# The MLP's second product, two token tiles at a time on the array's upper and lower 64 rows

## The chip, the cores and the metric

The kernel runs on one core of one Trainium2 chip. The metric is the device time of one execution, in microseconds. The kernel before takes 744.76 us, the median of three runs that lie between 744.68 and 744.93.

## The reference

Four layers act on `x` of 2048 tokens and 576 features, in bfloat16: linear attention (A), MLP (B), and both again with the same weights. Each adds to its input what it makes of the input's layer norm.

```python
def _B_ref(x, w1, b1, w2, b2):          # D = 576, F = 4608
    y = _layernorm(x, axis=-1)
    h = _gelu(jnp.einsum("bsd,df->bsf", y, w1) + b1)
    return jnp.einsum("bsf,fd->bsd", h, w2) + b2

x = x + _A_ref(_layernorm(x, axis=-1), A_wqkv, A_wo)
x = x + _B_ref(_layernorm(x, axis=-1), B_w1, B_b1, B_w2, B_b2)
x = x + _A_ref(_layernorm(x, axis=-1), A_wqkv, A_wo)
x = x + _B_ref(_layernorm(x, axis=-1), B_w1, B_b1, B_w2, B_b2)
```

The attention has 32 heads of 18 features. It takes keys, values and queries as products of `y` with `wqkv`, `phi(t) = where(t > 0, t + 1, exp(t)) + 1e-6` of keys and queries, sums keys times values over all tokens, and multiplies each query with that sum, over a denominator, and with `wo`.

## The kernel before

All weights stay in SBUF (`w1_sb`, `w2_sb` and so on; the profile calls both of the MLP's `w_sb`). Tokens stand in 16 tiles of 128; four tiles make a chunk of 512. The order on each engine is the order in which the program issues, kept by hand: `mm` (L228) chains TensorE's matmuls, and wrappers do the same for VectorE (`vec`), ScalarE (`act`), GpSimd (`pool`) and SyncE's DMA queue (`sp`). All TensorE work but the transposes is therefore under L229 in the profile, and all of the other engines' under L53; tiles tell the groups apart.

An MLP layer is `LayerB.run` (L1217). For each of four chunks it does:

- **The first product**, nine `m1_group`s (L1175) of four blocks of 128 hidden features. It works on half arrays: a matmul contracts over 64 partitions only, on the upper or the lower 64 rows of the array, and one of each half runs at the same time. 576 features are nine halves. `row_tiles` (L231) interleaves the two streams: the upper half takes the group's four sums in the order 0, 1, 2, 3, the lower half in the order 2, 3, 0, 1. The two halves must not write one PSUM bank at a time, so a bank passes from one to the other only after a *relay*, a tiny instruction on another engine (`relay_by_act`, a copy on ScalarE; or `relay_by_pool`, a memset on GpSimd) that waits for the last matmul of one half and is waited for by the first of the other. ScalarE's GELU writes a block into `units`, a buffer of 37 slots of 128 x 512; slot f is `hT[f]`. The sums 0 and 2 stand in a pair of banks (`hp_ps`, tags accA and accB in turn), the sums 1 and 3 in single banks (`h_ps`, tags one0 to one3 in turn).
- **The second product**, L1240 to L1277: tile by tile, 36 x 2 matmuls on the full array. The weights are a slot's 128 tokens (128 x 128), the moving operand is half a row of `w2_sb` (288 columns), and the result is `m_ps`, a pair of banks (two single banks, one2 and one3, for the last tile of a layer).

Between and beside these:

- `residual` (L546) adds the two halves to `xo`, the tile's `x` plus the bias, in one VectorE instruction. `bias_rows` (L537) makes `xo` on GpSimd; there is one buffer of it.
- `lnq` is a queue of layer norms for the next chunk's first product (kind B) and, where an attention follows, for the tiles just finished (kind A). `feed` puts a tile in, and each `tick` issues the next of four steps for every tile in it: statistics (VectorE), reciprocal root (GpSimd), the norm (VectorE, its padding on GpSimd), transposition through `shared` (VectorE, then after the fourth tile 16 DMAs into `yT`). Kind A also writes its rows to DRAM (`y_rows`).
- The second attention begins right after the first MLP layer with `lower_tails` (L652), which loads small tails into slots 17 and 18 of `units`; a GpSimd memset over slots 3 to 16; `placed_rows` (L496), DMAs of 12 tiles' rows into slots 3 to 16; `k_batch` (keys of two tiles) and `q_batch`, both with relays on GpSimd; and `key_rows` (L723), which needs a tile's rows as weights.
- `wo_pair` (L1025), an attention's last product, also works on half arrays, on two tiles at a time, with 288 columns.

In the second product, the full-array loop is:

```python
for f in range(NF):
    for half in range(2):
        mm(acc[half], hT[f][:, j * P:(j + 1) * P],
           w2_sb[:, f, half * HALF:(half + 1) * HALF], f == 0, f == NF - 1)
    if f % 12 == 6:
        while fed < {6: TPC - 1, 18: TPC}.get(f, 0):
            feed_next(c, fed)
            fed += 1
        lnq.tick()
```

The last tile of the last layer is computed as 384 and then 192 columns, so that the first part can be written out early.

Of the kernel before, what the change touches and what calls it, by code (L numbers as in the profile page):

```python
# [8 lines left out]
ALU = mybir.AluOpType  # L9
# [6 lines left out]
P = 128  # L16
NT = S // P
KD = 5
DPAD = KD * P
NF = F // P  # L20
# [6 lines left out]
NCB = S // CB  # L27
TPC = CB // P
CA = 512
NCA = S // CA  # L30
HALF = D // 2
# [4 lines left out]
def build(tc, A_x, A_wqkv, A_wo, B_w1, B_b1, B_w2, B_b2, out, n_layers=4):  # L36
    nc = tc.nc
    with ExitStack() as ctx:
# [23 lines left out]
        vec, act = InOrder(nc.vector, "VectorE"), InOrder(nc.scalar, "ScalarE")  # L62
        pool, sp = InOrder(nc.gpsimd, "GpSimd"), InOrder(nc.sync, "SyncE")

        x_in = A_x.flatten_outer_dims()
        out_f = out.flatten_outer_dims()
# [6 lines left out]
        def pair(name, tag=None):  # L73
            if tag is None:
                pair_turn["n"] += 1
                tag = ("accA", "accB")[pair_turn["n"] % 2]
            return ps_pair.tile([P, 2, 512], F32, name=name, tag=tag)
# [3 lines left out]
        def one_tag():  # L81
            one_turn["n"] += 1
            return f"one{one_turn['n'] % one_turn['banks']}"

        def one(name, tag=None):
            return ps_one.tile([P, 512], F32, name=name, tag=tag or one_tag())
# [106 lines left out]
        w2_sb = const.tile([P, NF, D], BF16, name="w2_sb")  # L193
        b1T = const.tile([P, NF], F32, name="b1T")
        b2_bc = const.tile([P, D], BF16, name="b2_bc")
        x_sb = const.tile([P, NT, D], BF16, name="x_sb")
# [25 lines left out]
        def pe(inst):  # L222
            if pe_last["last"] is not None:
                tc.add_manual_dep(inst.ins, pe_last["last"], NOSYNC, reason="TensorE order")
            pe_last["last"] = inst.ins.name
            return inst

        def mm(out_, lhsT, rhs, start, stop, **kw):  # L228
            return pe(nc.tensor.matmul(out_, lhsT=lhsT, rhs=rhs, start=start, stop=stop, **kw))  # L229

        def row_tiles(ops_of, dst, relay, after):  # L231


            order = [(hi, op) for step in zip([op for n in (0, 1, 2, 3) for op in ops_of(n, 0)],
                                              [op for n in (2, 3, 0, 1) for op in ops_of(n, 1)]) for hi, op in enumerate(step)]
            first, final, total = {}, {}, [0] * 4
            for i, (hi, (n, _, _)) in enumerate(order):
                first.setdefault((hi, n), i)
                final[(hi, n)] = i
                total[n] += 1  # L240
            relay_at = {max(final[(0, a)], final[(1, b)]): (a, b) for a, b in ((0, 2), (1, 3))}
            starts = {first[(1, 0)]: 0, first[(0, 2)]: 2, first[(1, 1)]: 1, first[(0, 3)]: 3}
            relay_of, seen = {}, [0] * 4
            for i, (hi, (n, wt, mv)) in enumerate(order):
                ins = mm(dst[n], wt, mv, seen[n] == 0, seen[n] == total[n] - 1)
                seen[n] += 1
                if i in starts:
                    tc.add_manual_dep(ins.ins, relay_of[starts[i]], SYNC, reason="row tiles take turns on a PSUM bank")
                if i in relay_at:
                    passed = relay()  # L250
                    tc.add_manual_dep(passed.ins, ins.ins.name, SYNC, reason="row tiles take turns on a PSUM bank")
                    for m in relay_at[i]:
                        relay_of[m] = passed.ins.name
                after(n, [a == b for a, b in zip(seen, total)], relay_at.get(i))
# [254 lines left out]
        class Queue:  # L509
# [3 lines left out]
            def feed(self, t, kind, eng="dve", transpose="dma"):  # L513
                n = Norm(t, kind, eng, transpose)
                self.items.append([n.stats, n.rstd, n.norm, n.transposed])
# [11 lines left out]
        lnq = Queue()  # L527

        def warm_table(func):
            act.activation(out=act_dummy[:, 0:1], in_=neg_half[:, 0:1], func=func)  # L530

        def two(ap):
            return ap.rearrange("p (h n) -> p h n", h=2)

        xo_of = {}

        def bias_rows(t):  # L537
            xo = work.tile([P, D], F32, name="xo", tag="xo", bufs=1)
            add = pool.tensor_tensor(out=xo[:], in0=x_sb[:, t, :], in1=b2_bc[:], op=ALU.add)
            if t == 0:  # L540
                tc.add_manual_dep(add.ins, gate["after"], SYNC, reason="not beside the attention's rows")
            xo_of[t] = xo
# [3 lines left out]
        def residual(li, t, halves):  # L546
            xo = xo_of.pop(t)[:] if t in xo_of else x_sb[:, t, :]
            vec.tensor_tensor(out=two(x_sb[:, t, :]), in0=halves, in1=two(xo), op=ALU.add)
            if li == n_layers - 1:
                sp.dma_start(out=out_f[t * P:(t + 1) * P, :], in_=x_sb[:, t, :])  # L550
# [619 lines left out]
        class LayerB:  # L1170
# [41 lines left out]
            def flush(self):  # L1212
                if self.held is not None:
                    self.held()
                    self.held = None

            def run(self):  # L1217
                li, next_kind = self.li, self.next_kind

                def feed_next(c, i):  # L1220
                    if c + 1 < NCB:
                        lnq.feed((c + 1) * TPC + i, "B")

                for c in range(NCB):

                    fed = 0
                    for g in range(self.done, NGRP):
                        self.m1_group(c, g)
                        if g in ((8,) if c == 0 else (5, 7)):
                            feed_next(c, fed)  # L1230
                            fed += 1
                        if g == (8 if c == 0 else 7):
                            bias_rows(c * TPC)
                        lnq.tick()
                    self.flush()
                    if c == NCB - 1 and next_kind == "A":
                        warm_table(ACT.Exp)
                    hT = self.hT.pop(c)
                    self.done = 0
                    for j in range(TPC):  # L1240
                        t = c * TPC + j
                        if t == NT - 1 and li == n_layers - 1:
                            for cols in (slice(0, 384), slice(384, D)):
                                width = cols.stop - cols.start
                                acc = one("m2_ps")
                                for f in range(NF):
                                    mm(acc[:, 0:width], hT[f][:, j * P:(j + 1) * P], w2_sb[:, f, cols],
                                       f == 0, f == NF - 1)
                                vec.tensor_tensor(out=x_sb[:, t, cols], in0=acc[:, 0:width],
                                                  in1=xo_of[t][:, cols], op=ALU.add)  # L1250
                                sp.dma_start(out=out_f[t * P:(t + 1) * P, cols], in_=x_sb[:, t, cols])
                            break
                        if t == NT - 1:

                            acc = [one("m2_ps", tag)[:, 0:HALF] for tag in ("one2", "one3")]
                        else:
                            both = pair("m2_ps")[:, :, 0:HALF]
                            acc = [both[:, half, :] for half in range(2)]
                        for f in range(NF):
                            for half in range(2):  # L1260
                                mm(acc[half], hT[f][:, j * P:(j + 1) * P],
                                   w2_sb[:, f, half * HALF:(half + 1) * HALF], f == 0, f == NF - 1)
                            if f % 12 == 6:
                                while fed < {6: TPC - 1, 18: TPC}.get(f, 0):
                                    feed_next(c, fed)
                                    fed += 1
                                lnq.tick()
                        if t == NT - 1:
                            for half in range(2):
                                cols = slice(half * HALF, (half + 1) * HALF)  # L1270
                                vec.tensor_tensor(out=x_sb[:, t, cols], in0=acc[half], in1=xo_of[t][:, cols], op=ALU.add)
                        else:
                            residual(li, t, both)
                        if j + 1 < TPC:
                            bias_rows(t + 1)
                        if next_kind == "A":
                            lnq.feed(t, "A")  # L1277

        kinds = ["A", "B", "A", "B"][:n_layers]

# [153 lines left out]
```

## Time and profile before

| | |
|---|---|
| median of three runs | 744.76 us (744.68 to 744.93) |
| the profiled execution | 745.07 us |
| its span, first to last instruction | 743.4 us |
| TensorE matmuls busy | 737.0 us, 6942 instructions |
| TensorE weight loads busy | 479.2 us, 6951 instructions |
| VectorE, ScalarE, GpSimd busy | 268.8, 297.3, 131.7 us |
| `m_ps` (second product): matmuls of 128 x 288 | 2216 of `units` and 16 of `pk`, mean 286 ns, and 72 of 384 and 192 columns |
| `h_ps` and `hp_ps` (first product) | 2592 of 64 x 512, mean 376 ns |
| `m_ps` in the chain that ended last | 38% of the span |

The profile gives a matmul's duration from its start to the modelled end of its results, so neighbours overlap: the mean of one is not the time between two. The time between two is had from starts, or from the length of a stretch over its count. The chain (section 4 of the page) follows the work that ended last back from the end; listed in order of time it shows stretches of the same work with start, length and count. Form `64*128` means a weight tile of 64 rows and 128 columns, half the array; `128*128` is the full array.

### The profile page before, as it was taken

The numbers are of one execution on the slowest core, as the hardware profiler recorded it, in microseconds if no ns is written. First come the engines' busy times: TensorE is split into PE (matmuls) and PEld (weight loads), VectorE is DVE, ScalarE is ACT, GpSimd is POOL, SyncE is SP. The second block draws the span as 40 slices with busy tenths as digits, with TensorE's granted clock in tenths as the row PEclk, the third lists the DMA queues.
The fourth block names the chain that finished last, engine by engine and source line by source line (L and its number), as shares of the span: only waits on it lengthen the run. The fifth ranks groups of instructions, "written<-read, shape, count | busy, mean of one in ns | idle before, by whom it ended". The sixth has DMA issues, their size and how long they took to land.

```text
span 743.4 us, 16663 instructions
## 1 busy us (share of the span) xinstructions
PE 737.0 (99%) x6942; PEld 479.2 (64%) x6951; DVE 268.8 (36%) x674; ACT 297.3 (40%) x642; POOL 131.7 (18%) x403
## 2 busy tenths in 40 slices
PE   8999999999999999999999999999999999999998
PEld 4666557774576457646777665777646754774476
DVE  7868735433025302400365685452401040100000
ACT  5666743007601740374035666320373047106700
POOL 4541000422022201200213120021300120010010
PEclk9999999999999999999999999999999999999999
DMA  7956220022011202110023001202000200020000
GB/s 197 240 161 210 66 86 17 16 46 44 2 27 42 38 1 45 36 26 1 17 85 85 28 1 38 67 1 53 18 1 9 52 10 1 18 44 9 1 10 24
DMA packets 61297, 34.74 MB, mean 47 GB/s; under 512 B 37126, under 2 KB 61222, under 8 KB 61222
## 3 DMA queue, kind: packets, MB, share of 16 engines
q1 hardware_dynamic: 60470, 33.45, 17.8%
q8 instruction: 54, 0.88, 0.5%
q10 hardware_dynamic: 752, 0.23, 0.2%
q14 instruction: 21, 0.17, 0.1%
HBM read 21.70 MB, written 4.93 MB: 36 GB/s over the span
## 4 chain that ended last, share of the span: by engine, by line
PE 98%; DVE 1%; DMA 1%; SPq 0%; issue 0%; DVEq 0%
PE m_ps L229 38%; PE hp_ps L229 20%; PE h_ps L229 17%; PE k_ps L229 5%; PE q_ps L229 5%; PE wo_ps L229 5%; PE rk_ps L229 4%; PE tp L468 1%; PE side_ps L229 1%; DMA x_sb<-in_A_x_dram 1%; SPq L53 0%; PE den_ps L229 0%; PE kvwo_ps L229 0%; PE kv_ps L229 0%; PE rden_ps L229 0%; DVE pk L53 0%
## 5 line engine op out<-in xcount | busy, mean ns | idle before, releaser
L229 PEld LDWEIGHTS <-units 128*128 128x128 bf16 (+1 forms) x2926 | 267.4, 97 | 66.4 <-issue 3.6
L229 PE MATMUL m_ps<-w_sb,units 128*128 128x288 bf16 (+2 forms) x2288 | 283.0, 286 | 0.0
L229 PEld LDWEIGHTS <-w_sb 64*128 64x128 bf16 x2304 | 129.2, 94 | 129.8 <-issue 2.1
L229 PE MATMUL h_ps<-yT,w_sb 64*128 64x512 bf16 x1152 | 173.7, 376 | 0.0
L229 PE MATMUL hp_ps<-yT,w_sb 64*128 64x512 bf16 x1152 | 151.5, 376 | 0.0
L53 DVE TENSOR_TENSOR x_sb<-m_ps,xo 128x576 bf16<-128x576 f32 (+3 forms) x34 | 24.4, 721 | 323.6 <-PE m_ps L229 323.6
L53 ACT ACTIVATE units<-hp_ps,b1T 128x512 bf16<-128x512 f32 x144 | 91.2, 684 | 86.4 <-PE hp_ps L229 86.4
L53 ACT COPY relay_sb<-relay_sb 128x1 f32<-128x1 f32 x112 | 21.4, 191 | 235.7 <-PE hp_ps L229 225.0
L53 ACT ACTIVATE units<-h_ps,b1T 128x512 bf16<-128x512 f32 x142 | 95.2, 687 | 0.0
L53 POOL TENSOR_TENSOR xo<-x_sb,b_bc 128x576 f32<-128x576 bf16 x32 | 40.8, 1274 | 302.9 <-DVE x_sb L53 291.5
L229 PE MATMUL k_ps<-wkv_sb,yT 64*128 64x288 bf16 (+3 forms) x432 | 61.0, 299 | 0.6 <-ACT yT L53 0.5
L229 PE MATMUL hp_ps<-yT,w_tail 64*128 64x512 bf16 x144 | 54.1, 376 | 0.0
L229 PE MATMUL h_ps<-yT,w_tail 64*128 64x512 bf16 x144 | 54.1, 376 | 0.0
L53 DVE BATCH_NORM_STATS2 ln_st<-x_sb 128x6 f32<-128x288 bf16 x128 | 51.3, 441 | 1.4 <-DMA x_sb<-in_A_x_dram 1.1
L53 DVE STREAM_TRANSPOSE shared<-y_ring 128x640 bf16<-128x640 bf16 x40 | 32.9, 826 | 41.4 <-DMA yT<-shared 39.3
L53 ACT ACTIVATE phi_e<-k_ps 128x288 bf16<-128x288 f32 x64 | 26.3, 413 | 53.7 <-PE k_ps L229 50.0
L229 PEld LDWEIGHTS <-yT 64*128 64x128 bf16 (+1 forms) x448 | 36.3, 95 | 9.2 <-ACT yT L53 0.8
L229 PE MATMUL q_ps<-yT,wq_sb 64*128 64x512 bf16 (+2 forms) x273 | 40.4, 347 | 0.4
L53 DVE TENSOR_SCALAR y_ring<-x_sb,ln_mv,ln_rstd 128x576 bf16<-128x576 bf16 (+2 forms) x60 | 30.3, 506 | 24.5 <-POOL ln_rstd L53 24.3
L53 POOL MEMSET pool_relay<- 128x1 f32 x152 | 16.7, 110 | 125.3 <-PE hp_ps L229 43.6
L229 PE MATMUL wo_ps<-shared,units 64*128 64x288 bf16 (+1 forms) x480 | 38.1, 283 | 0.1
L229 PEld LDWEIGHTS <-w_tail 64*128 64x128 bf16 x288 | 27.1, 94 | 16.7
(110 smaller groups left out, 500.4 us busy)
## 6 DMA issues: line engine op xcount, KB each, us to landing
yT<-shared SPq DMA_DIRECT2D x160, 40.0 KB
w_sb<-in_B_w_dram SPq DMA_DIRECT2D x12, 432.0 KB
w_sb<-in_B_w_dram SPq DMA_DIRECT2D x9, 512.0 KB
yT<-rden_rows SPq DMA_DIRECT2D x24, 126.0 KB
y_rows<-y_ring SPq DMA_DIRECT2D x16, 144.0 KB
units<-y_rows SPq DMA_DIRECT2D x16, 144.0 KB
x_sb<-in_A_x_dram SPq DMA_DIRECT2D x15, 144.0 KB
out_dram<-x_sb SPq DMA_DIRECT2D x15, 144.0 KB
```

Of the source, the lines that this page charges most:

```text
L53: inst = issue(*args, **kw)
L229: return pe(nc.tensor.matmul(out_, lhsT=lhsT, rhs=rhs, start=start, stop=stop, **kw))
L468: pe(nc.tensor.transpose(out=tp[:, k - a, :], in_=self.y[:, k * P:(k + 1) * P], identity=ident[:]))
```

## The change

The second product runs through `row_tiles` too: a new `two_tiles` takes tiles t and t + 1 together. Sum n is tile n % 2 and column half n // 2; each sum is made of 36 matmuls on the upper and 36 on the lower 64 rows, so that a call has 288 half-array matmuls in four quarters, with two relays on ScalarE. The even tile's two sums stand in a pair of banks and are complete after three quarters; its residual is issued there. The odd tile's stand in two single banks and are complete at the end; they are added in two VectorE instructions. The `lnq` feeds and ticks are counted in matmuls of a call. In the last call of a layer, slots 17, 18 and 3 to 16 are read first, and its ticks stand at other places. In the last chunk of the last layer only the first two tiles are paired; the other two stay as they were.

```diff
+            def two_tiles(self, c, j, hT, feed):
+                li, t = self.li, c * TPC + j
+                both = pair("m2_ps")
+                tags = ("one2", "one3") if t + 2 == NT else (None, None)
+                early = [one("m2_ps", tag) for tag in tags]
+                dst = [both[:, 0, 0:HALF], early[0][:, 0:HALF], both[:, 1, 0:HALF], early[1][:, 0:HALF]]
+                step = dict(n=0)
+                early_slots = [17, 18] + list(range(3, 17)) if t + 2 == NT else []
+                order = early_slots + [f for f in range(NF) if f not in early_slots]
+
+                def ops_of(n, hi):
+                    at, rows, cols = (j + n % 2) * P, slice(64 * hi, 64 * hi + 64), slice(n // 2 * HALF, (n // 2 + 1) * HALF)
+                    return [(n, hT[f][rows, at:at + P], w2_sb[rows, f, cols]) for f in order]
+
+                def after(n, done, turn):
+                    step["n"] += 1
+                    if step["n"] == 72:
+                        feed()
+                    if step["n"] % 48 == 24 and (step["n"] < 216 or t + 2 < NT):
+                        lnq.tick()
+                    if n in (0, 2) and done[0] and done[2]:
+                        residual(li, t, both[:, :, 0:HALF])
+                        bias_rows(t + 1)
+                        if self.next_kind == "A":
+                            lnq.feed(t, "A")
+                    if step["n"] in (224, 244, 264) and t + 2 == NT:
+                        lnq.tick()
+
+                row_tiles(ops_of, dst, relay_by_act, after)
+                xo = xo_of.pop(t + 1)
+                for half in range(2):
+                    cols = slice(half * HALF, (half + 1) * HALF)
+                    vec.tensor_tensor(out=x_sb[:, t + 1, cols], in0=dst[1 + 2 * half], in1=xo[:, cols], op=ALU.add)
+                if li == n_layers - 1:
+                    sp.dma_start(out=out_f[(t + 1) * P:(t + 2) * P, :], in_=x_sb[:, t + 1, :])
+                if (j + 2) < TPC:
+                    bias_rows(t + 2)
+                if self.next_kind == "A":
+                    lnq.feed(t + 1, "A")
...
-                    for j in range(TPC):
+                    last = li == n_layers - 1 and c == NCB - 1
+                    for j in range(0, 2 if last else TPC, 2):
+                        self.two_tiles(c, j, hT, lambda: [feed_next(c, i) for i in range(fed, TPC)] if j == 0 else None)
+
+                    for j in range(2, TPC if last else 2):
                         t = c * TPC + j
...
-                        if t == NT - 1:
-
-                            acc = [one("m2_ps", tag)[:, 0:HALF] for tag in ("one2", "one3")]
-                        else:
-                            both = pair("m2_ps")[:, :, 0:HALF]
-                            acc = [both[:, half, :] for half in range(2)]
+                        both = pair("m2_ps")[:, :, 0:HALF]
                         for f in range(NF):
                             for half in range(2):
-                                mm(acc[half], hT[f][:, j * P:(j + 1) * P],
+                                mm(both[:, half, :], hT[f][:, j * P:(j + 1) * P],
                                    w2_sb[:, f, half * HALF:(half + 1) * HALF], f == 0, f == NF - 1)
-                            if f % 12 == 6:
-                                while fed < {6: TPC - 1, 18: TPC}.get(f, 0):
-                                    feed_next(c, fed)
-                                    fed += 1
-                                lnq.tick()
-                        if t == NT - 1:
-                            for half in range(2):
-                                cols = slice(half * HALF, (half + 1) * HALF)
-                                vec.tensor_tensor(out=x_sb[:, t, cols], in0=acc[half], in1=xo_of[t][:, cols], op=ALU.add)
-                        else:
-                            residual(li, t, both)
-                        if j + 1 < TPC:
-                            bias_rows(t + 1)
-                        if next_kind == "A":
-                            lnq.feed(t, "A")
+                        residual(li, t, both)
+                        bias_rows(t + 1)
```

## The prediction, made before the changed kernel ran

> **What bounds the kernel now.** I read the page of the profile first: busy shares, clock row, chain.
>
> ```profile
> PE 737.0 (99%) x6942; PEld 479.2 (64%) x6951; DVE 268.8 (36%) x674; ACT 297.3 (40%) x642; POOL 131.7 (18%) x403
> ...
> PEclk9999999999999999999999999999999999999999
> ...
> PE 98%; DVE 1%; DMA 1%; SPq 0%; issue 0%; DVEq 0%
> ```
>
> TensorE is the chain from end to end, at full granted clock in every slice. A busy PE is not PE at its peak, so the next question is at which pace its matmuls follow each other. For that I read the chain in order of time (start, us, what).
>
> ```profile
> 113.39 4.41 PE wo_ps L229 x72
> ...
> 129.97 35.39 PE m_ps L229 x288
> 165.36 1.18 PE hp_ps L229 x9
> 167.41 1.08 PE hp_ps L229 x9
> ...
> 198.49 1.08 PE hp_ps L229 x9
> 200.43 35.38 PE m_ps L229 x288
> ```
>
> One whole round of the MLP, 512 tokens, is 200.43 - 129.97 = 70.46 us: 288 full-array matmuls of 288 columns (second product), then nine groups of the first product on half arrays. Inside the groups the `hp_ps` rows come every (198.49 - 167.41) / 16 = 1.9425 us, and there are two to a group, so nine groups at that pace are 34.97 us. The first group is off the pace: 165.36 to 167.41 is 2.05. The wo pairs are the kernel's sample of the new form: 72 half-array matmuls of 288 columns, two at a time, in 4.41 us. That is 122.5 ns for each two (I call this a slot).
>
> Where the first product hands over to the second, the timeline has:
>
> ```profile
> 129.60 0.38 PE L229 MATMUL h_ps<-yT,w_tail 64*128 64x512 bf16 x1
> 129.91 0.54 PE L229 MATMUL m_ps<-w_sb,units 128*128 128x288 bf16 x3
> ```
>
> A 512-column pair is followed by the next after 1.9425 / 9 = 0.216 us; here the next starts after 0.31. So about 0.09 us go where half arrays change to the full one.
>
> **The change part by part.** *Removed and added matmuls.* 30 of the 32 tile passes are paired (15 calls of `two_tiles`), all but the last two of the last layer. Out go 30 x 72 = 2160 full matmuls, in come 4320 half ones, 2160 slots. The full ones cost at most 35.39 / 288 = 122.9 ns with the change of form in it, the slots 122.5 by the wo pairs: no gain from packing, since all 4608 contraction rows already filled the array. What differs is only the change of form. A round without it is 34.97 + 288 x 0.1225 = 34.97 + 35.28 = 70.25 us against 70.46: **0.21 us for one change in and one out** (0.09 in by the timeline, the other 0.12 behind it and on the way out). Eight second products have eight ways in and, the last being the end, seven ways out. Afterwards only the last still changes, between tiles 13 and 14. So seven of each go: 7 x 0.21 = **1.5 us**, 1.4 to 1.6 by the rounding of the rows.
> The Trainium skill (TensorEngine Tiling (Array Packing), Key Properties) says that changing the tiling mode drains TensorE; the 0.31 against 0.216 agrees.
>
> *Twice the weight loads.*
>
> ```profile
> L229 PEld LDWEIGHTS <-units 128*128 128x128 bf16 x288 | 28.1, 98 | 7.5 <-issue 0.4
> ...
> L229 PEld LDWEIGHTS <-units 64*128 64x128 bf16 x69 | 4.1, 94 | 0.2
> ```
>
> The first row is a second product (200.4 to 235.7), the second a wo pair (113.3 to 117.8). A half load takes 94 ns, no less than a full one, and there are two to a slot: 188 ns of loads in 122.5. They fit because the two halves load at once: the wo pairs hold the pace with them. I take 0. If they queued, it would be 2160 x (188 - 122.5) = 141 us.
> The Trainium skill (TensorE: Matmul & The Clock Gate, LDWEIGHTS) speaks against the change: a load's time is its columns over 1.2 GHz, whatever the rows, so half the rows save nothing; two in turn at its 107 ns would add 2160 x 91 ns = 196 us (estimate). The 94 ns row agrees on one load and the 4.41 us row excludes the turns.
>
> *A longer stretch at this density.* A wo pair is 4.4 us; a second product is 35. The nearest long stretch is the second attention's key rows (windows of one token tile each; PE busy, count, and so on):
>
> ```profile
> 397.29:399.57 2.28, 2.28 (x43) 1.78 (x41) 1.23 (x4) 1.19 (x5) 0.80 (x7) 1.00 0.40 64
> 399.57:401.84 2.27, 2.27 (x43) 1.77 (x41) 1.23 (x4) 1.18 (x5) 0.80 (x7) 1.00 0.25 38
> ```
>
> There a tile issues 36 half matmuls (18 keys, 8 main, 10 side; the counts take in the neighbours' overlap) in 2.275 us, 63 ns apart, for some 20 us; the new form needs 61. The paces above, 216 ns for 512 columns and 122.5 for 288, make 0.417 ns a column and 2.5 ns a matmul; at that the tile's columns need 2.238 us. So the stretch loses at most 1.6%, and that with POOL's relays (most of its x7) in its path. Bounds for 15 x 144 x 0.1225 = 264.6 us: 0 to 4.3 us. I take 0, the wo row being the same shape.
>
> *Relays.* Each call adds two copies on ACT (0.19 us) that let a bank pass from one half to the other. Each stands ready from the end of a quarter (36 slots, 4.41 us) and is needed a quarter later; behind it ACT has only the next relay and, a product later, the GELUs. Cost 0. Where that cover is short, in wo pairs (4.5 slots), the first lost 4.50 - 4.41 = 0.09 us; 30 relays so would lose 2.7.
>
> *GELU to matmul.* The first quarter reads all 36 units in 4.4 us, not 8.8. Group eight's last GELU ends 1.6 us into the product (130.27 + 1.27 against 129.91), and is needed 35 x 0.1225 = 4.3 us in: covered. w2 is in SBUF by 80 us (the trace's DMA packets).
>
> *Residuals, xo, norms.* The even tile's residual moves to 75% of a call, the odd one's to the end, as two adds of some 0.45 us instead of one of 0.76; its banks are wanted 4.9 us later, in group 1. The only `xo` buffer is refilled (1.27 us on POOL) in the 4.4 us between. The next chunk's norms come at one go, ahead of the residual, and have over 20 us. All 0.
>
> *Into the second attention.* Here steps move past POOL and SP:
>
> ```profile
> 368.79 1.27 POOL L53 TENSOR_TENSOR xo<-x_sb,b_bc 128x576 f32<-128x576 bf16 x1 [5.48 <-DVE x_sb L53]
> 370.49 0.22 POOL L53 TENSOR_SCALAR ln_u<-ln_mv 128x1 f32<-128x1 f32 x1 [0.43 <-DVE ln_mv L53]
> 370.79 0.56 POOL L53 TENSOR_TENSOR ln_rstd<-ln_u,neg_half 128x1 f32<-128x1 f32 x1
> 371.88 0.24 POOL L53 COPY y_ring<-y_ring 128x64 bf16<-128x64 bf16 x1 [0.53 <-DVE y_ring L53]
> 372.05 0.15 POOL L53 MEMSET units<- 128x12 bf16 x1
> ...
> 372.39 0.53 SPq L53 DMA_DIRECT2D units<-wkv_sb  x1
> ...
> 373.68 10.70 SPq L53 DMA_DIRECT2D units<-y_rows  x10
> ```
>
> The product ends at 376.6 (call it T). Units 17 and 18 are read first in the last quarter, so the key tail still loads at T - 4.2. Units 3 to 16 come free 20 slots before the end, T - 2.4 instead of T - 4.6: the first row DMA moves from T - 2.9 to T - 2.3. The memset waits behind tile 14's norm on POOL, whose residual now comes at T - 4.2: residual to statistics 1.9 us (0.76 and three rows of the statistics), rstd 0.9, norm and pad copy 1.0, so T - 0.2 instead of T - 4.5. The second row DMA waits for it (was T - 2.2), behind it the other rows, then tile 14's and 15's. The first rows take 1.6 us each to land, so the train is 0.6 to 1.0 us later. By the semaphores, row 1 lands at 379.5 and TensorE wants it at 383.5; the later ones have 2.9 us or more. Cost 0; beyond 2.9 us late, TensorE waits. Behind the memset on POOL stands k_batch's first relay, wanted at T + 0.9: 1 us to spare.
>
> **Sum.** The profiled execution took 745.07 us, 743.4 of it span: 745.07 - 1.5 = 743.6. The median of the runs is 0.31 below that execution: **743.3 us**.
>
> **The rivals.**
> 1. *Slower: the density doesn't hold over 35 us.* For: no stretch before issues two loads and two matmuls per 122.5 ns for longer than 4.4 us, and the one that comes near loses 1.6%. Against: those tiles have relays on their path. Price up to 4.3 - 1.5 = +2.8, 747.5 us. It decides from 0.7 ns per slot (1.5 us / 2160).
> 2. *The saving is given back at bank changes or at the attention.* 30 relays at 0.05 us, half the 0.09 row, are 1.5 us, and a row train 4.4 us late would cost as much: 744.8 us. Against: 4.2 us of cover for the one, 2.9 for the other.
> 3. *Loads in turn* (141 us slower, 884 us); the wo row speaks against it.
> 4. *It does not do what it says:* the full form stays somewhere. The order of instructions after the change has full `m_ps` matmuls only for the last two tiles, so no.
> 5. *A little more than the sum:* the rounds' rows allow 0.23 each, 1.6 us, and the skew between halves some 0.04 at each way out: 742.9 us.
>
> **Chances.** Forecast 0.62; rival 1 0.14; rival 2 0.13; rival 3 0.02; rival 4 none; rival 5 0.09. A measurement of this kernel can tell about 0.2%, 1.49 us; the line is 743.27, and the forecast (its own range 743.1 to 743.5) sits on it. So its 0.62 is split evenly: faster 0.31 + 0.09 = 0.40; same 0.31 + 0.07 of rival 2 = 0.38; slower 0.22, rivals 1 and 3 and the 0.06 of rival 2 that overshoots. The range from 742.7 (rival 5 and the spread of the runs) to 746.0 takes in rival 2 and the near half of rival 1.
>
> **What the profile after would show.** Right: no step of 0.31 between `h_ps` and `m_ps` but once, after tile 13 of the last chunk; rounds of 70.25 us; `m_ps` half matmuls two to 122.5 ns in all four quarters; the chain still on PE. Rival 1: `m_ps` stretches over 35.4 us with even gaps above 122.5. Rival 2: gaps at a quarter's start, or PE waiting for `units<-y_rows` or POOL behind T. Wrong altogether: a half load that starts only where the other ends.

## The result and the profile after

The changed kernel takes 743.41 us (median of 20 runs, 743.1 to 743.8), the kernel before 744.79 (20 runs, 744.56 to 745.47). The ratio is 0.9981, with a 95% interval of 0.9974 to 0.9988: 1.38 us less. The profiled execution took 743.2 us, 741.5 of it span (before 745.07 and 743.4).

The page of the changed kernel: TensorE's busy time, its clock and its share of the chain.

```profile
PE 735.5 (99%) x9102; PEld 571.2 (77%) x9111; DVE 270.2 (36%) x688; ACT 302.8 (41%) x672; POOL 131.9 (18%) x403
...
PEclk9999999999999999999999999999999999999999
...
PE 98%; DVE 1%; DMA 0%; issue 0%; POOL 0%; DVEq 0%
```

TensorE is still the whole chain at full clock; there are 2160 more matmuls and as many more weight loads. The chain in order of time (start, us, what), the same places as before:

```profile
129.57 35.28 PE m_ps L229 x576
164.85 1.04 PE hp_ps L229 x9
...
166.79 1.04 PE hp_ps L229 x9
...
199.82 35.28 PE m_ps L229 x576
...
703.04 35.40 PE m_ps L229 x432
```

A round is 199.82 - 129.57 = 70.25 us (before 70.46). The product itself is 35.28, which is 288 slots of 122.5 ns with nothing over. Its first group of the first product is on the pace too: 164.85 to 166.79 is 1.94, where it was 2.05. The timeline at the way in:

```profile
129.19 0.38 PE L229 MATMUL h_ps<-yT,w_tail 64*128 64x512 bf16 x1
129.37 1.51 PE L229 MATMUL m_ps<-w_sb,units 64*128 64x288 bf16 x21
```

The step of 0.31 us is gone: 0.18 here, and the second half of that first pair follows 0.04 later, together the 0.216 of any 512-column pair. Only the last product (703.04) keeps a change, since its last two tiles stay on the full array: 35.40, 0.12 above the others.

The chain of before has its last product here:

```profile
704.92 35.40 PE m_ps L229 x288
```

The chain's first `m_ps` to its last gives the account: 704.92 - 129.97 = 574.95 before, 703.04 - 129.57 = 573.47 after, **1.48 us** less. The other 0.4 us of the 1.9 us between the two spans lie ahead of the first MLP product, where nothing is changed: in the execution before, VectorE waited 0.39 us for a tile of `x` at 8.27 us, which in the execution after had come by 7.86. The medians, 1.38 apart, don't show them.

### The profile page after: what moved, and what is told of

Same layout as the page of the kernel before. It is cut to its first block, busy times and chain, and to the rows that moved or that the text cites. A ratio compares the mean times of both kernels' runs of the same rounds, so it can differ in the third digit from the quotient of the medians.

```text
span 741.5 us, 21075 instructions
## 1 busy us (share of the span) xinstructions
PE 735.5 (99%) x9102; PEld 571.2 (77%) x9111; DVE 270.2 (36%) x688; ACT 302.8 (41%) x672; POOL 131.9 (18%) x403
## 4 chain that ended last, share of the span: by engine, by line
PE 98%; DVE 1%; DMA 0%; issue 0%; POOL 0%; DVEq 0%
PE m_ps L229 38%; PE hp_ps L229 20%; PE h_ps L229 18%; PE k_ps L229 5%; PE q_ps L229 5%; PE wo_ps L229 5%; PE rk_ps L229 4%; PE tp L468 1%; PE side_ps L229 1%; DVE ln_st L53 0%; PE den_ps L229 0%; PE kvwo_ps L229 0%; PE kv_ps L229 0%; DMA x_sb<-in_A_x_dram 0%; PE rden_ps L229 0%; DVE pk L53 0%
## 5 line engine op out<-in xcount | busy, mean ns | idle before, releaser
L229 PEld LDWEIGHTS <-units 64*128 64x128 bf16 (+1 forms) x5070 | 321.3, 94 | 12.0 <-issue 0.5
L229 PE MATMUL m_ps<-w_sb,units 64*128 64x288 bf16 (+2 forms) x4432 | 284.0, 283 | 0.0
L229 PEld LDWEIGHTS <-w_sb 64*128 64x128 bf16 x2304 | 158.4, 94 | 95.8 <-issue 0.7
L229 PE MATMUL h_ps<-yT,w_sb 64*128 64x512 bf16 x1152 | 169.6, 376 | 0.0
L229 PE MATMUL hp_ps<-yT,w_sb 64*128 64x512 bf16 x1152 | 155.5, 376 | 0.0
L53 DVE TENSOR_TENSOR x_sb<-m_ps,xo 128x288 bf16<-128x288 f32 (+3 forms) x48 | 25.3, 554 | 336.7 <-PE m_ps L229 336.7
L53 ACT COPY relay_sb<-relay_sb 128x1 f32<-128x1 f32 x142 | 27.2, 191 | 261.8 <-PE m_ps L229 176.6
L53 POOL TENSOR_TENSOR ln_rstd<-ln_u,neg_half 128x1 f32<-128x1 f32 x64 | 36.5, 570 | 8.6 <-DVE ln_u L53 3.6
L53 DVE TENSOR_SCALAR y_ring<-x_sb,ln_mv,ln_rstd 128x576 bf16<-128x576 bf16 (+2 forms) x60 | 28.3, 479 | 24.0 <-POOL ln_rstd L53 23.7
```

The costliest lines, as they stand in the source:

```text
L53: inst = issue(*args, **kw)
```

## The experiments

All have the changed kernel as their start, unless the text says otherwise. The question was first where the 1.5 us come from (one price per change of form, and nothing else), then whether each cost put at nothing is nothing because it is covered, and by how much.

**Half of the changes back.** In the first three chunks of each MLP layer tiles 0 and 1 stay paired, and tiles 2 and 3 are computed on the full array: six rounds have one change in and out again.

```diff
-                    for j in range(0, 2 if last else TPC, 2):
+                    paired = 2 if last or c < NCB - 1 else TPC
+                    for j in range(0, paired, 2):
                         self.two_tiles(...)
-                    for j in range(2, TPC if last else 2):
+                    for j in range(paired, TPC):
...
```

> In six of the eight rounds (all chunks but the last of each layer) only tiles 0 and 1 are paired; tiles 2 and 3 run on the full array, with the ticks of before. So those rounds have one change of form in and one out again, but half of their matmuls in the new form. Theory (all of the gain is the change of form, 0.212 us for one in and one out): 743.41 + 6 x 0.212 = 744.7 us, and rounds of 70.46 us in the trace, as before. Rival (the gain comes with the half-array matmuls, their order of sums or the moved residuals and norms, in proportion): half of six sevenths of the 1.4 us come back, 744.0 us, rounds of 70.35.

Measured 744.74 us (11 runs), ratio to the kernel before 0.9999 (0.9990 to 1.0008). Half of the paired tiles of six rounds are still there, and the gain is gone: what counts is whether a product changes form, not how many tiles are paired. The chain has the product with the change inside:

```profile
129.78 35.39 PE m_ps L229 x432
```

35.39 again, as before, and its rounds are 200.24 - 129.78 = 70.46 us again. Over the whole chain this run keeps 0.21 us of the 1.48, 704.52 - 129.78 = 574.74 against 574.95: one product, the last of the first MLP layer, still has no change of form.

**The price by itself.** Ten times in each of the 15 calls, a small extra product into a spare bank stands between two slots (its result is not used): one full matmul of 128 columns, or, as control, two half matmuls of 128 columns side by side.

```diff
...
+                def extra_product():
+                    if not extra:
+                        extra["at"] = one("sw_ps", spare_tags[0])
+                    a = extra["at"]
+                    mm(a[:, 0:P], ident[:], w2_sb[:, 0, 0:P], True, True)
...
                 def after(n, done, turn):
                     step["n"] += 1
+                    if 80 <= step["n"] <= 260 and step["n"] % 20 == 0:
+                        extra_product()
```

The control's product:

```diff
+                    a, b = extra["at"]
+                    mm(a[:, 0:P], ident[0:64, :], w2_sb[0:64, 0, 0:P], True, True)
+                    mm(b[:, 0:P], ident[64:P, :], w2_sb[64:P, 0, 0:P], True, True)
```

> Each of the 15 calls of two_tiles gets ten extra matmuls of 128 columns on the full array, into a bank that nobody reads, each between two slots of half matmuls: 150 extra matmuls and 150 changes of form in and out. An extra matmul by itself takes 128 x 0.417 + 2.5 = 56 ns. Theory (a change in and out costs 0.212 us wherever it stands): 743.41 + 150 x (0.056 + 0.212) = 783.6 us. Rival (the change is cheap and most of the gain came otherwise, say 0.1 us): 766.8 us or less.

> The control of the run before: at the same 150 places two extra half matmuls of 128 columns, one on each half, in place of the full one. The same time of columns, no change of form. Theory: 743.41 + 150 x 0.056 = 751.8 us. Rival (an extra instruction costs by itself, by its weight load or by breaking the order): as much as the run before.

Measured 783.6 us with the full ones and 751.89 with the halves (two runs each). Both stream the same columns; the difference, 31.7 us over 150 changes in and out, is **0.211 us for each**. The timeline of the kernel with the full ones splits it:

```profile
139.06 1.40 PE L229 MATMUL m_ps<-w_sb,units 64*128 64x288 bf16 x20
140.39 0.23 PE L229 MATMUL sw_ps<-w_sb,ident 128*128 128x128 bf16 x1
140.55 1.40 PE L229 MATMUL m_ps<-w_sb,units 64*128 64x288 bf16 x20
```

Ten slots are 1.225 us, and the full matmul starts 1.33 after their first: 0.105 on the way in. Its own 128 columns at the prediction's pace take 0.056, and the next half starts after 0.16: 0.10 on the way out. Each way costs about half. At both, the first matmul of the new form starts 0.07 us before the modelled end of the old form's last (140.39 against 139.06 + 1.40, 140.55 against 140.39 + 0.23), where two matmuls of 288 columns of one form overlap by 0.16 (0.283 long, 0.1225 apart). So most of the price is overlap that is lost; how far the array must be empty at a change, no run here shows.
The Trainium skill (TensorEngine Tiling (Array Packing), Key Properties) has the drain at a change of tiling mode but no price; these runs agree, and give it as some 0.105 us a way.

**Four loads to a slot.** Each half matmul of 288 columns is cut in two of 144, with a weight load each.

```diff
...
-                    at, rows, cols = (j + n % 2) * P, slice(64 * hi, 64 * hi + 64), slice(n // 2 * HALF, (n // 2 + 1) * HALF)
-                    return [(n, hT[f][rows, at:at + P], w2_sb[rows, f, cols]) for f in order]
+                    at, rows, base = (j + n % 2) * P, slice(64 * hi, 64 * hi + 64), n // 2 * HALF
+                    return [(n, hT[f][rows, at:at + P], (slice(q, q + HALF // 2), w2_sb[rows, f, base + q:base + q + HALF // 2]))
+                            for f in order for q in (0, HALF // 2)]
...
```

The counts at which feeds and ticks stand are doubled with it.

> Each half matmul of two_tiles is split into two of 144 columns, each with its own weight load: four weight loads and four matmuls where there were two of each. Theory (weight loads of the two halves and of matmuls that follow each other lie over each other, the columns set the pace): two slots of 144 x 0.417 + 2.5 = 62.5 ns for one of 122.5, 2160 x 2.5 ns = +5.4 us, 748.8 us. Rival (each half takes its own loads one after the other, 94 ns each): 188 ns for 122.5, +141 us, 885 us. Second rival (all loads one after the other): 376 ns for 122.5, +548 us, 1291 us.

Measured 748.98 us (two runs), ratio 1.0056 (1.0037 to 1.0074). The windows view, same stretch of a second product (us, PE busy, PEld busy and their counts, then the other engines), first the changed kernel, then this one:

```profile
200.00:235.00 35.00, 35.00 (x576) 35.00 (x572) 7.86 (x17) 2.13 (x7) 6.56 (x11) 1.00 0.05 13
```

```profile
200.00:235.00 35.00, 35.00 (x1108) 34.76 (x1106) 7.86 (x17) 3.17 (x8) 6.25 (x11) 1.00 0.06 16
```

1106 loads of 94 ns (the groups view of this stretch) would be 104 us in turn; they fit into 35, so by these rows three are under way at a time. Every load has the same 94 ns in them, so that is the time of one and not the pace at which loads can follow each other. The product is 36.00 us in the chain, 0.72 or 2.5 ns a slot longer: the fixed part of a matmul, as the prediction had it from the rows. Loads are no bound here, at twice the density of the change.

**Rows read last.** The last call before an attention reads slots 3 to 16 at the end of each quarter instead of early, so that the row DMAs of the second attention are let go later still.

```diff
-                order = early_slots + [f for f in range(NF) if f not in early_slots]
+                order = early_slots[:2] + [f for f in range(NF) if f not in early_slots] + early_slots[2:]
```

> In the last call of the first MLP layer slots 3 to 16 are read last instead of right behind 17 and 18, so that the second attention's row DMAs can start only at the product's end T: the first one at T + 0.2 us instead of T - 2.7, the second at T + 0.8 instead of T - 0.4; the train is 1.2 to 2.4 us later. In the trace of the changed kernel row 1 lands 2.8 us before it is wanted and the last rows 2.0 us. Theory (that slack is real): 743.4 to 743.9 us, TensorE waiting at most 0.4 us for rows. Rival (the rows were already at the edge, so each us later is a us lost): 744.6 to 746.3 us.

Measured 743.6 us (743.16 to 743.73, 11 runs), ratio 0.9982 (0.9973 to 0.9990). But the rows moved less than was expected. The timeline of SyncE's queue, first the changed kernel, then this one:

```profile
372.69 14.75 SPq L53 DMA_DIRECT2D units<-y_rows  x12
```

```profile
374.00 13.97 SPq L53 DMA_DIRECT2D units<-y_rows  x12
```

The first row DMA is 1.3 us later and still 1.4 us ahead of T, since the slots come free one by one as the last quarter reads them. The second, which in both kernels stands behind GpSimd's memset over these slots (T - 0.5 and T - 0.4), moves by 0.1 us, and the last of the twelve ends 0.5 us later (387.97 against 387.44). By the semaphores the rows land 0.5 to 0.6 us later, only the very first 1.2, and not 1.2 to 2.4. The attention behind it is as long as before, 116.73 us against 116.72 in the chains, so that much of the rows' slack is real; the rest of the 2.0 us is read from the semaphores and was not tried.

**More relays, less cover.** The sums are built in pieces: four of 9 slots (180 more relays, a relay has 1.1 us until it is needed), or twelve of 3 slots (660 more, 46 in each call; 0.37 us).

```diff
+                def pieces(ops_of, dst, relay, after):
+                    size = NF // 4                                  # or NF // 12
...
+                    for b in range(4):                              # or 12
+                        for q in range(4):
+                            nu, nl = q, (q + 2) % 4
...
-                row_tiles(ops_of, dst, relay_by_act, after)
+                pieces(ops_of, dst, relay_by_act, after)
```

> The four sums of a call are made in four pieces of 9 slots each instead of one of 36, so that banks change hands four times as often: 14 relays to a call for 2, 180 more in all, each with a cover of 9 slots, 1.1 us. Theory (a relay that is ready in time costs nothing): 743.4 us. Rival (each change of bank costs about 0.05 us): 743.4 + 180 x 0.05 = 752.4 us.

> The same in twelve pieces of 3 slots: 46 relays to a call, 690 in all, with a cover of 3 slots, 0.37 us. In the trace before, from the slot's end of the last matmul of one half to the end of ScalarE's copy are some 0.4 us, and the next matmul must still be released: a way of 0.5 to 0.6 us. Theory (a relay costs what its way is longer than its cover): 690 x 0.13 to 0.23 = 90 to 160 us, 833 to 903 us. Rival (each change of bank costs 0.05 us, covered or not): 743.4 + 660 x 0.05 = 776 us.

Measured 750.14 us (749.0 to 750.37) for pieces of 9, a miss: neither 743.4 nor 752.4. Pieces of 3 took 817.2 us (one run), between the two theories. In the second the relays cost plainly. The timeline of ScalarE in one of its products:

```profile
210.84 0.19 ACT L53 COPY relay_sb<-relay_sb 128x1 f32<-128x1 f32 x1 [0.18 <-PE m_ps L229]
211.36 0.19 ACT L53 COPY relay_sb<-relay_sb 128x1 f32<-128x1 f32 x1 [0.33 <-PE m_ps L229]
211.73 0.19 ACT L53 COPY relay_sb<-relay_sb 128x1 f32<-128x1 f32 x1 [0.18 <-PE m_ps L229]
```

Three slots are 0.367 us; the relays come 0.52 and 0.37 apart in turn, so two relays lose 0.15 us. A product takes 43.4 us instead of 35.28, 8.1 over 92 relays, 0.09 each. In the run with pieces of 9 there is nothing of that kind: seven of its eight products take as long as without pieces. All that was lost lies at one place, the last product of the first MLP layer (1.2 us in its first quarter, 1.09 between its two calls) and the attention behind it (121.35 us from its first `k_ps` to the next layer's first `m_ps`, where the changed kernel has 116.72: 4.6). The waits of TensorE there:

```profile
PE q_ps L229 <- POOL pool_relay L53: 2.7, 1, 2.7
...
PE m_ps L229 <- ACT relay_sb L53: 1.0, 1, 1.0
PE m_ps L229 <- DVE x_sb L53: 0.9, 1, 0.9
```

So my theory had the relays right and the edit wrong: with pieces, a call's even tile is complete 1.1 us before the call's end instead of 4.4, and what hangs on its residual moves with it. Three places were tested one by one.

**Pieces everywhere but in the last call before the attention.**

```diff
...
+                if t + 2 == NT and self.next_kind == "A":
+                    row_tiles(ops_of, dst, relay_by_act, after)
+                else:
+                    pieces(ops_of, dst, relay_by_act, after)
```

> Pieces of nine slots in 14 of the 15 calls, 168 more relays with 1.1 us of cover each; the last call before the second attention stays in quarters of 36. Theory (the relays cost nothing; all 6.7 us of the run with pieces everywhere came in that one call and the attention behind it, because there the even tile's residual moves from 4.4 us to 1.1 us before the end): 743.4 us, 743.2 to 743.9. Rival (the pieces themselves cost, some 6.7 / 15 us in a call): 743.4 + 14 x 0.45 = 749.7.

Measured 744.58 us (744.3 to 744.93), ratio 0.9995 (0.9987 to 1.0004): 5.6 of the 6.7 us are gone, and 1.2 are left over the changed kernel, which the theory did not have. They are the first quarter of tiles 12 and 13. The timeline of ScalarE there, this kernel and then the changed one:

```profile
341.97 1.28 ACT L53 ACT_TABLE_LOAD   x1
...
343.37 0.40 ACT L53 COPY relay_sb<-relay_sb 128x1 f32<-128x1 f32 x2
```

```profile
341.88 1.28 ACT L53 ACT_TABLE_LOAD   x1
...
344.81 0.19 ACT L53 COPY relay_sb<-relay_sb 128x1 f32<-128x1 f32 x1 [1.43 <-PE m_ps L229]
```

Behind the layer's last GELU ScalarE loads the table for the attention, 1.28 us, and the first relays of this product stand behind it. In the changed kernel the load is done 1.4 us before the relay's turn; with pieces two relays were ready and waited.

The 1.09 us between the two calls are gone too, though tile 13's adds, which wait for `xo`, come as late in this run as in the other (360.36 and 360.20 us): in quarters the last call wants their banks 4.4 us after its start, in pieces after 1.1. That loss took both, the late adds and the early need.

> As the run with pieces of nine slots in all calls but the last before the second attention, but that layer's last call but one (tiles 12 and 13) is back in quarters of 36 as well: 13 calls in pieces, 156 more relays of 1.1 us cover. Theory (the 1.2 us left over there were the first relay of tiles 12 and 13, which stands on ScalarE behind the table load for the attention, 1.28 us, issued once behind the layer's last GELU; everywhere else the relays cost nothing): 743.4 us, 743.2 to 743.8. Rival (the relays or pieces cost something in each call): 744.4 us.

```diff
-                if t + 2 == NT and self.next_kind == "A":
+                if t >= NT - TPC and self.next_kind == "A":
```

Measured 743.51 us (743.09 to 743.83, 11 runs), ratio 0.9982 (0.9973 to 0.9991): nothing is left. 156 relays with 1.1 us of cover cost nothing, and the table load was the rest.

**Only the residual late.** No pieces; tile 14's residual, its `xo` and its norm are issued later, 1.1 us or 3.4 us before the product's end instead of 4.4.

```diff
-                    if n in (0, 2) and done[0] and done[2]:
+                    late = t + 2 == NT and self.next_kind == "A"
+                    if step["n"] == 270 if late else n in (0, 2) and done[0] and done[2]:    # 270, or 232
                         residual(li, t, both[:, :, 0:HALF])
```

> The changed kernel with quarters of 36 slots; only tile 14's residual, its next input on GpSimd and its norm before the second attention are issued 54 matmuls later, 1.1 us instead of 4.4 us before the product's end. Theory (the handover to the second attention stands on GpSimd's order: its first relay and then the relays of the queries queue behind what hangs on this residual): the attention loses the 4.6 us that it lost with pieces everywhere, 743.4 + 4.6 = 748.0 us, and the product itself nothing. Rival (that loss came from the pieces): 743.4 us.

> The same residual issued 16 matmuls later, 3.4 us before the end instead of 4.4. In the order of instructions tile 14's norm then stands behind tile 15's two adds on VectorE (they end 1.0 us after the product's end T), and its padding copy on GpSimd ahead of the first relay of the keys: norm to T + 1.4, copy to T + 1.7, relay at T + 1.75 where it was issued at T + 0.84. Theory (the first relay has no more than 1 us to spare, and TensorE waits for the rest of what it is late): 0 to 0.9 us, 743.4 to 744.3. Rival (the handover has no slack at all behind its start, and the queries' relays are late too, as with 3.3 us): 746 us or more.

Measured 746.13 us with the residual 1.1 us before the end (10 runs, 745.82 to 747.45; ratio 1.0020, 1.0011 to 1.0030), and 744.34 with 3.4 us (10 runs, 744.11 to 744.71; 0.9993, 0.9984 to 1.0002). The timelines of GpSimd around the product's end (375.3 to 375.4 in all three): the changed kernel, the residual 3.4 us and 1.1 us before the end.

```profile
374.86 0.15 POOL L53 MEMSET units<- 128x12 bf16 x1
376.22 0.10 POOL L53 MEMSET pool_relay<- 128x1 f32 x1 [1.21 <-PE k_ps L229]
...
379.13 0.10 POOL L53 MEMSET pool_relay<- 128x1 f32 x1
```

```profile
376.89 0.24 POOL L53 COPY y_ring<-y_ring 128x64 bf16<-128x64 bf16 x1 [2.67 <-DVE y_ring L53]
377.06 0.25 POOL L53 MEMSET pool_relay<- 128x1 f32 x2
```

```profile
381.39 0.37 POOL L53 COPY y_ring<-y_ring 128x64 bf16<-128x64 bf16 x1 [2.10 <-DVE y_ring L53]
381.70 0.25 POOL L53 MEMSET pool_relay<- 128x1 f32 x2
```

In the changed kernel GpSimd stands idle for 1.2 us before the first relay of the keys (376.22). With the residual 1 us later, tile 14's padding copy gets in front of it, and the relay comes at 377.06, 1.7 us after the product's end, as worked out; the attention is 0.93 us longer in the trace. With the residual 3.3 us later, that copy stands in front of the queries' relay instead (381.70 against 379.13) and itself waits 2.1 us for tile 14's norm on VectorE; the attention is 2.5 us longer, the product not at all. The theory's mechanism holds, its 4.6 us were too much: in the run with pieces tile 15's adds also waited for `xo`, 1.0 us more, which put the norms and the relay behind them later still. That part was read from the trace of that run, not tried by itself.

## Why the prediction was right, point by point

- **What bounds it, and the pace.** TensorE from end to end, slots of 122.5 ns: measured 35.28 us for 288 slots, as summed. No gain from packing, as said.
- **The change of form, 0.21 us, seven times.** Measured 0.21 by the rounds, 0.211 by the 150 extra changes; 1.48 us in the trace for the 1.5 of the sum. Its inner split, 0.09 in and 0.12 for the rest, was rough: it is about 0.105 each way. The forecast of 743.3 us stands 0.1 below the median measured. The 1.38 us measured lie just short of the 1.49 that the prediction called its line between faster and the same; on which side of it the result fell was, by its own account, near to even odds.
- **Twice the loads at 0.** Right, and not narrowly: the run with four loads to a slot has the same pace but for 2.5 ns. Rival 3 (in turn) is out. By its own rows a half load is a little shorter than a full one, 94 ns to 98. The Trainium skill's time for one load of 128 columns (TensorE: Matmul & The Clock Gate, LDWEIGHTS), 107 ns, lies above both; the 196 us that came of laying such loads end to end are refuted by the windows above. The Trainium skill's other rule, that tiles of the array load and multiply independently (TensorEngine Tiling (Array Packing), Key Properties), is the one that the runs bear out.
- **Density at 0 of up to 4.3.** Every product keeps 122.5 ns a slot over its whole length, so rival 1's 747.5 us had no ground. That what those key rows lose belongs to their relays was argued and not tried.
- **Relays at 0.** Right at 4.4 us of cover, and still at 1.1. But the working missed an instruction: "behind it ACT has only the next relay and, a product later, the GELUs" leaves out the table load behind the last GELU of the layer, which is in the trace of before. In tiles 12 and 13 the cover is 1.4 us, not 4.2. That nothing came of it was luck, since the step had not looked. Rival 2's price for a short relay, 0.05 to 0.09 us, is what pieces of 3 slots showed (0.09).
- **Residuals, `xo`, norms at 0.** Right where they are. The step looked at each by itself; that tile 13's adds (through the one `xo` buffer) and tile 14's norm both hang on the even tile's residual, and are late when it comes 3.3 us later, came out only when pieces moved it.
- **Into the second attention at 0.** The direction and sizes held: memset at T - 0.5 (predicted T - 0.2), first row DMA at T - 2.7 (T - 2.3). By the semaphores row 1 landed 2.8 us before it was wanted (4.0 before the change) and tile 12's, the tightest of the last four, 2.0 (2.9): slack went down by 0.9 to 1.2 us, for the 0.6 to 1.0 worked out, and TensorE waits for none, here or with the rows 0.5 us later. "1 us to spare" ahead of the keys' first relay was 1.2, and the run with the residual 1 us later shows what is behind it.
- **The others.** Rival 2 (all given back, 744.8) did not happen, but the late-residual runs show that its second mechanism, a handover that comes too late, begins within 1 us. The first quarters of all products have 36 even slots, so the GELUs were covered. Rival 4 is out by the timeline. Rival 5's 742.9 had 0.23 a change; it is 0.21.

## What to carry to other kernels

When a product switches between the full array and half arrays, count the switches, not the matmuls: each way had the same price at every place measured here (about 0.105 us), so where the neighbours run on half arrays, pairing some of a product's tiles is worth nothing and pairing all of them is worth one price in and out. Before costing a moved step at nothing, list what stands in front of each instruction that releases the bound engine, table loads too, and note the time to spare; here it was 1.2 us at the tightest, and an edit that moved one residual by 3.3 us cost twice what the change had gained.

## What the runs showed of the hardware that was not expected

- **Loads overlap more than two at a time.** 1106 half-array loads of 94 ns lay in a stretch of 35 us, 3.0 under way on average and 1.5 in each half, beside matmuls that kept their 62.5 ns.
- **A bank's hand-over by a copy on ScalarE** is free with 1.1 us of cover and costs 0.09 us with 0.37 us.
- **Both ways of a change of form cost**, about 0.105 us in and as much out. The way out stood in the trace of before as well:

```profile
164.83 0.53 PE L229 MATMUL m_ps<-w_sb,units 128*128 128x288 bf16 x3
165.29 0.60 PE L229 MATMUL hp_ps<-yT,w_sb 64*128 64x512 bf16 x4
```

The third full matmul starts two paces of 0.1225 behind 164.83, at 165.08, and the first half one 0.22 later instead of 0.12.
